# Moving the block loads of chunks 6 and 7 ahead of an output-weight load on the DMA-issuing queue

## The chip, the cores and the metric

The kernel runs on one core of a Trainium2 chip. The core has five engines that run side by side, each through its own list of instructions in order: TensorE (PE; its weight loads appear as PEld), VectorE (DVE), ScalarE (ACT), GpSimd (POOL) and SyncE (SP), which here does nothing but issue DMA transfers. The metric is the device time of one execution in microseconds (us). Less is better.

## What is computed

```python
def _attn_ref(q, k, v):                      # 8 batches, 8 heads, 576 positions, 64 per head
    scores = scale * np.matmul(q, k.transpose(0, 1, 3, 2))
    Dmat = np.where(rel >= 0, gamma[:, None, None] ** rel[None, :, :], 0.0)
    ret = scores * Dmat[None, :, :, :]
    return np.matmul(ret, v).astype(np.float32)

def _moe_ref(x, w1, w2, w3, w_out):          # x: 4608 x 512, w1..w3: 512 x 768, w_out: 768 x 512
    h = np.maximum(np.maximum(x @ w1, x @ w2), x @ w3)
    return (h @ w_out).astype(np.float32)
```

The first part is a retention layer: attention scores without softmax, with a weight that decays with distance by a factor of the head. Its output, with the heads side by side, is the input x of a feed-forward layer that takes the maximum of three products and multiplies it by w_out. The four weights arrive as 64-bit floating-point numbers; the kernel turns them into 32-bit numbers itself.

## The kernel before, in words

**Tiling.** The 4608 rows are cut into 36 chunks of 128 rows, and four chunks make one feed-forward tile of 512 rows, so there are nine tiles. While `ffn(t)` works on the feed-forward tile `t`, the retention steps of the four chunks of tile `t + 1` are woven in. `steps(t + 1)` returns twelve lists of steps, called places here. The loop at the bottom of the kernel runs the steps of one place and then lets `ffn(t)` go on to its next `yield`. There is no automatic scheduling: the order in which these Python functions are called is the order of each engine's instructions.

**The first tile.** Only the first tile, `ffn(0)`, is touched by this change. Its up products run in nine units of two halves each (`up_plain`, PE line 858, four double-pass matmuls of 128x512 a half), and after place n comes unit n. While these run, the weights are converted (`convert`, 12 pairs of pieces: nine pairs of w1 to w3, then three pairs of w_out). A pair needs, in this order, ACT lines 695 and 696, DVE line 703 with ACT lines 702 and 704, then DVE lines 708, 713 and 728. Each raw pair lies in one of four buffers (`bits`); the conversion of a pair ends with the load of further pieces (`load_weights`), which waits for a buffer whose DVE line 713 is done. After the up products come the down products with w_out (`downs_plain`, PE line 845).

**The chunks 4 to 7**, which `steps` calls a, b, c and d, are the ones prepared during `ffn(0)`. What happens to one chunk:

- `load(g, "kv")` issues two DMAs on SP (line 247): `kraw` and `vraw`, 256 KB each.
- `load_blocks(g, 0, 1, 2, 3)` issues sixteen DMAs on SP (line 229): eight 32 KB pieces of `qraw`, then eight of `kxraw`. They write 32x32 blocks in places such that one VectorE transpose of 32x32 blocks turns the chunk. There are two buffers of each, so chunk 7 takes that of chunk 5.
- `transposes(g)` is two DVE instructions (line 216), `kT<-kxraw` and then `qT<-qraw`.
- `decay(g)` multiplies the values by their decay. For chunks 4 and 5 it is one DVE instruction (line 254). For chunks 6 and later it is eight ACT instructions, one a head (line 204, `vraw<-vraw,gk`), put in a list called `scaling` from which `scale(3)` takes three after each half unit.
- `scores(g)` calls `chunk_scores`: for each head, PE line 322 (`sk`, needs `kT` and `qT`) and PE line 325 (`kv`, needs `kraw` and the scaled `vraw` of that head). Before it, whatever is left in `scaling` is issued.
- `values([a, b])` multiplies on (PE lines 439 and 446) and gives the input of the next tile.

**Order around the change.** The second half of unit 8 is followed by `scores(6)`, `scores(7)` and the down products. The sixteen ACT multiplications of chunks 6 and 7 thus go to the ACT queue in groups of 3, 3, 3, 3, 3 and 1, between the conversion's instructions: the third group has the last two of chunk 6 and the first of chunk 7, and the last group has the eighth head of chunk 7 alone.

**SP's queue.** All transfers are issued by SP in order. Each DMA carries one of eight semaphores in turn, so SP does not issue a DMA before the one eight places ahead of it has landed. A DMA that must wait for a buffer holds up all behind it.

## Time and profile before

| what | value |
|---|---|
| median of 3 runs | 740.69 us (738.68 to 741.06) |
| the profiled execution's own time | 739.48 us |
| its span in the profile | 737.8 us |
| PE busy | 731.2 us (99%) |
| DVE busy | 575.3 us (78%) |
| ACT busy | 352.2 us (48%) |
| SP's DMA queue | 58.76 MB, 35.3% of 16 DMA engines |

The span is the time from the first to the last instruction in the profile; 1.7 us of the execution lie around it. Busy times are sums over the whole span, and most of the span is not like the stage that the change touches, which lies between 58 and 96 us. So the stage is read on its own, from the timelines of SP, ACT, DVE and PE. In a timeline a row gives the start in us, the duration, the engine, the line, the operation, what it writes and reads, and how many equal ones stand together ("x8"); "SPq" is SP's issuing. In the chain of work that ended last, a row "DMA kxraw<-in_k_dram" is the time from the issue of that transfer to its landing.

### The profile page before, as it was taken

The page shows a single profiled execution, that of the slowest core. Times are in us where ns is not written, and L with a number is a line of the kernel's source. Part 1 is how long each engine was busy: PE and PEld are TensorE (multiplying, and loading weights), DVE is VectorE, ACT ScalarE, POOL GpSimd, SP SyncE. Part 2 cuts the span into 40 slices and gives each one's busy share as a digit, 9 for nine tenths or more (in the row PEclk, how much of TensorE's full clock was granted, in tenths as well). Part 3 has the DMA queues.
Part 4 walks back from the last instruction along what each step waited for, and adds up shares of the span by engine and source line. Part 5 has one row for each costly group of instructions (what it writes and reads, how often), then busy time and mean ns, then how long its engine had stood idle before and what let it go on. Part 6 is the DMA issues. An engine that isn't in the chain of part 4 may idle for free.

```text
span 737.8 us, 17257 instructions
## 1 busy us (share of the span) xinstructions
PE 731.2 (99%) x6916; PEld 604.5 (82%) x6916; DVE 575.3 (78%) x1050; ACT 352.2 (48%) x734; POOL 37.1 (5%) x43
## 2 busy tenths in 40 slices
PE   9999999999999999999999999999999999999998
PEld 7644546888888888888888888888888888888887
DVE  4899799999886895689658876787768966893676
ACT  4795905554345524544354535543555255424441
POOL 2000010112000100010000000000100010000000
DMA  9878544414251415141424243322514151000001
GB/s 234 270 225 248 113 85 119 83 27 92 70 103 23 95 40 105 36 84 48 102 51 77 47 109 60 65 52 59 114 26 91 44 106 26 1 29 30 1 1 57
DMA packets 234832, 59.90 MB, mean 81 GB/s; under 512 B 220672, under 2 KB 228864, under 8 KB 234752
## 3 DMA queue, kind: packets, MB, share of 16 engines
q1 hardware_dynamic: 233776, 58.76, 35.3%
q8 instruction: 54, 0.88, 0.5%
q14 instruction: 26, 0.21, 0.1%
q10 hardware_dynamic: 976, 0.04, 0.1%
HBM read 49.32 MB, written 9.44 MB: 80 GB/s over the span
## 4 chain that ended last, share of the span: by engine, by line
PE 91%; SPq 5%; DMA 2%; DVE 1%; issue 0%; DVEq 0%
PE a L833 20%; PE b L833 17%; PE c L833 9%; PE di L666 7%; PE d L833 6%; PE e L833 6%; PE dhc L666 5%; PE up L858 3%; PE deg L666 3%; SPq L229 3%; PE sk L322 3%; PE down L845 3%; PE o L439 2%; PE o L446 2%; PE dfd L666 2%; PE dx L573 1%
## 5 line engine op out<-in xcount | busy, mean ns | idle before, releaser
L821 DVE TENSOR_TENSOR part<-part 128x512 f32<-128x512 f32 x168 | 117.8, 701 | 85.9 <-ACT part L818 83.3
L818 ACT COPY part<-b 128x512 f32<-128x512 f32 x120 | 70.3, 586 | 163.2 <-PE b L833 162.7
L821 DVE TENSOR_TENSOR h<-h,part 128x512 f32<-128x512 f32 x120 | 83.2, 694 | 23.8 <-ACT h L818 19.8
L204 ACT ACTIVATE vraw<-vraw,gk 128x64 f32<-128x64 f32 x240 | 77.0, 347 | 11.3 <-DMA vraw<-in_v_dram 11.3
L818 ACT COPY part<-a 128x512 f32<-128x512 f32 x96 | 56.3, 586 | 51.5 <-PE a L833 51.1
L833 PE MATMUL b<-s,n 128*128 128x256 f32 x288 | 73.9, 379 | 0.0
L858 PE MATMUL up<-xT,w 128*128 128x512 f32 (+2 forms) x160 | 62.9, 552 | 0.0
L833 PEld LDWEIGHTS b<-s,n 128*128 128x128 f32 x288 | 54.7, 190 | 7.4
L858 PEld LDWEIGHTS up<-xT,w 128*128 128x128 f32 x160 | 28.8, 190 | 31.5 <-issue 28.6
L339 POOL TENSOR_TENSOR s<-s,gs_of 64x512 f32<-64x512 f32 x24 | 26.4, 1101 | 552.3 <-DVE s L337 512.1
L833 PE MATMUL c<-xT,w 128*128 128x256 f32 x192 | 51.3, 389 | 0.0
L655 ACT COPY k<-di 128x256 f32<-128x256 f32 x49 | 18.3, 373 | 68.5 <-PE di L666 42.1
L833 PE MATMUL d<-s,w 128*128 128x256 f32 x192 | 49.8, 380 | 0.0
L833 PE MATMUL b<-xT,n 128*128 128x256 f32 x192 | 49.3, 379 | 0.0
L833 PE MATMUL a<-xT,w 128*128 128x256 f32 x192 | 49.3, 379 | 0.0
L833 PE MATMUL a<-s,w 128*128 128x256 f32 x192 | 49.3, 379 | 0.0
L833 PE MATMUL a<-xT,n 128*128 128x256 f32 x192 | 45.4, 379 | 0.0
L833 PE MATMUL e<-xT,w 128*128 128x256 f32 x192 | 45.4, 379 | 0.0
L833 PEld LDWEIGHTS e<-xT,w 128*128 128x128 f32 x192 | 36.5, 190 | 5.4 <-issue 0.5
L833 PEld LDWEIGHTS b<-xT,n 128*128 128x128 f32 x192 | 36.5, 190 | 5.0
L833 PEld LDWEIGHTS a<-xT,n 128*128 128x128 f32 x192 | 36.5, 190 | 5.0
L833 PEld LDWEIGHTS a<-xT,w 128*128 128x128 f32 x192 | 36.5, 190 | 5.0
(183 smaller groups left out, 1378.6 us busy)
## 6 DMA issues: line engine op xcount, KB each, us to landing
bits<-in_moe_w_dram SPq DMA_DIRECT2D x9, 1024.0 KB, 7.9
kraw<-in_k_dram SPq DMA_DIRECT2D x32, 256.0 KB, 3.1
vraw<-in_v_dram SPq DMA_DIRECT2D x32, 256.0 KB, 3.9
qraw<-in_q_dram SPq DMA_DIRECT2D x256, 32.0 KB, 2.1
kxraw<-in_k_dram SPq DMA_DIRECT2D x256, 32.0 KB, 2.1
out_dram<-osb SPq DMA_DIRECT2D x56, 128.0 KB, 1.7
bits<-in_moe_w_out_dram SPq DMA_DIRECT2D x6, 512.0 KB, 6.0
out_dram<-osb SPq DMA_DIRECT2D x7, 256.0 KB, 2.0
```

The lines of the kernel that those rows point to most:

```text
L204: scaling.popleft()()
L229: nc.sync.dma_start(t[r:r + 32, :, e, :], src[b, :, pos:pos + 32, 32 * a:32 * a + 32].rearrange("h p i -> p h i"))
L322: nc.tensor.matmul(s[half(c), h, :], lhsT=kT[half(c), h, :], rhs=qT[half(c), h, :], start=True, stop=True)
L339: nc.gpsimd.tensor_tensor(new, new, factor, op=ALU.mult)
L439: nc.tensor.matmul(o[m][half(c), n, u, :], lhsT=vds[g][half(m), h, :], rhs=sts[g][half(m), h, :], start=n == 0 and u == 0, stop=place(g, m ...
L655: nc.scalar.copy(place, a)
L666: nc.tensor.matmul(banks[chain], lhsT=hidden(h, order, b, late_ones)[:, e], rhs=late["V"][v][:, e], start=begins and e == 0, stop=chain no ...
L818: nc.scalar.copy(of[step], ps[step[0]][:])
L821: nc.vector.tensor_tensor(of[dst], a, b, op=op)
L833: nc.tensor.matmul(ps[chain][:, e, :], lhsT=factor(w, 2 * fp + e), rhs=xS[t][x], start=n == 1 and e == 0, stop=ends, skip_group_check=True)
L845: nc.tensor.matmul(b[:], lhsT=h[:, fb, m * P:(m + 1) * P], rhs=w_sb["out", fb], start=fb == blocks[0], stop=fb == blocks[-1])
L858: nc.tensor.matmul(ps[:, a:b], lhsT=w_sb[i, fb][:, dc * P:(dc + 1) * P], rhs=xT[t][:, dc, a:b], start=dc == 0 and a == 0, stop=dc == NDC - ...
```

## The change

The sixteen-DMA block loads of chunks 6 (c) and 7 (d) are moved to the fifth place. Chunk 6's stand at its beginning, ahead of the chunk's own `load`; chunk 7's stand at its end, behind chunk 5's transposes.

```diff
             at(4, (transposes, a))
-            at(5, (load, c, "kv"), (decay, b), (transposes, b))
-            at(6, (load, d, "kv"), (decay, c), (load_blocks, c, 0, 1, 2, 3))
-            at(7, (values, [a, b]), (decay, d), (convert, 2), (load_blocks, d, 0, 1, 2, 3))
+            at(5, (load_blocks, c, 0, 1, 2, 3), (load, c, "kv"), (decay, b), (transposes, b), (load_blocks, d, 0, 1, 2, 3))
+            at(6, (load, d, "kv"), (decay, c))
+            at(7, (values, [a, b]), (decay, d), (convert, 2))
             at(8, (transposes, c))
```

The lists of PE, DVE, ACT and POOL stay the same, instruction for instruction. On SP the order becomes (two DMAs to a pair of w_out or to a `kraw` and `vraw`, sixteen to a set of blocks):

```
before: w_out pair 1 | kv 6 | w_out pair 2 | kv 7 | blocks 6 | w_out pair 3 | blocks 7 | blocks 8 ...
after:  w_out pair 1 | blocks 6 | kv 6 | blocks 7 | w_out pair 2 | kv 7 | w_out pair 3 | blocks 8 ...
```

## The prediction

> **What bounds the kernel now.** I read the page's chain first, then PE's waits over the whole span, then the chain and the timelines between 58 and 96 us.

> ```profile
> ## 4 chain that ended last, share of the span: by engine, by line
> PE 91%; SPq 5%; DMA 2%; DVE 1%; issue 0%; DVEq 0%
> ```

> PE carries the chain; 5% of it is SP's issuing. PE's list of waits says where PE is idle, and from 22 us on it has one entry:

> ```profile
> PE sk L322 <- DVE qT L216: 1.8, 1, 1.8
> ```

> It is the start of `scores(7)`. Everything else PE does behind 22 us stands back to back, so this stage can give back at most 1.8 us, and whatever holds PE here longer is added whole: from 95.42 us the chain is PE alone, matmul behind matmul. The chain (start, duration, what) shows what the 1.8 us come from:

> ```profile
> 81.65 4.72 DMA bits<-in_moe_w_out_dram
> ...
> 90.20 2.31 DMA kxraw<-in_k_dram
> ...
> 92.59 0.71 DVE kT L216
> 93.30 0.60 DVE qT L216
> ```

> The blocks of chunk 7 are issued last of their kind, behind w_out's third pair; the last lands at 92.5, and DVE, idle for 3.1 us before it, transposes. SP's timeline gives the queue:

> ```profile
> 59.15 0.92 SPq L516 DMA_DIRECT2D bits<-in_moe_w_out_dram  x2
> 60.11 0.67 SPq L247 DMA_DIRECT2D kraw<-in_k_dram  x1
> 60.89 1.54 SPq L247 DMA_DIRECT2D vraw<-in_v_dram  x1
> 62.97 4.03 SPq L516 DMA_DIRECT2D bits<-in_moe_w_out_dram  x2
> 67.09 0.38 SPq L247 DMA_DIRECT2D kraw<-in_k_dram  x1
> 67.51 1.47 SPq L247 DMA_DIRECT2D vraw<-in_v_dram  x1
> 69.03 6.65 SPq L229 DMA_DIRECT2D qraw<-in_q_dram  x8
> 75.72 5.39 SPq L229 DMA_DIRECT2D kxraw<-in_k_dram  x8
> 81.21 0.87 SPq L516 DMA_DIRECT2D bits<-in_moe_w_out_dram  x2
> 82.13 4.58 SPq L229 DMA_DIRECT2D qraw<-in_q_dram  x8
> 86.75 3.90 SPq L229 DMA_DIRECT2D kxraw<-in_k_dram  x8
> ```

> SP issues without a pause here, so what is moved forward pushes back what it passes. The change moves 32 issues past two w_out pieces and the `kraw` and `vraw` of chunk 7 (and sixteen of them past those of chunk 6). So the question is who uses these four, and when. `vraw` of chunk 7 lands 6.5 us after its issue at 67.51 (the answer on that one issue), at 74.1. Its first user is on ACT:

> ```profile
> 80.91 0.81 ACT L204 ACTIVATE vraw<-vraw,gk 128x64 f32<-128x64 f32 x3
> 81.63 1.13 ACT L695 ACTIVATE expo<-bits 128x1024 f32<-128x1024 bf16 x1
> 82.67 1.25 ACT L696 ACTIVATE mant<-bits,one 128x1024 f32<-128x1024 uint32 x1
> ...
> 89.65 0.35 ACT L204 ACTIVATE vraw<-vraw,gk 128x64 f32<-128x64 f32 x1
> ```

> The third multiplication of the first row, near 81.4, is chunk 7's first head; the last row, done at 90.0, is its eighth. Between them ACT is never idle: 8.6 us of work in a fixed order, conversion and multiplications alternating. PE's last `kv` matmuls of `scores(7)` need the eighth. The cover of `vraw` 7 is thus 81.4 - 74.1 = 7.3 us on ACT's side.

> **The change, part by part.** Nothing is computed that was not before, and only SP's order differs. I follow SP's clock.

> *Blocks 6 forward.* They come right behind w_out's first pair (59.15, 59.65). There is no wait for their buffer: chunk 4's transposes end at 53.9 (53.20 + 0.67, DVE). The situation is that of 81.21 in the queue above: seven issues go out, the eighth waits for the second w_out piece to land (eight semaphores), and the `kxraw` take 3.9. That piece lands 7.1 us after 59.65, at 66.7 as before. So the `kxraw` go from 67.1 to 71.0.

> *`kraw` and `vraw` 6 back,* from 60.11 and 60.89 to 71.1 and 71.6. Where they follow blocks elsewhere (99.59 and 100.09) they take 0.40 and 0.53 and land 3.0 and 3.4 us later: `vraw` 6 lands at 75.0. ACT wants it at 72.33, so ACT is 2.6 us late. Cover: the conversion of the last up pair, which has its weights ready at 78.1 (DVE line 728, 76.83 + 1.23) for a unit that PE starts at 84.1 (91.1 less 7.0); 2.4 us late it is still 3.6 us early. Cost on PE: nothing.

> *Blocks 7 forward.* They wait for chunk 5's transposes, which end at 61.8; SP gets there at 72.2, so the wait costs nothing, and what is queued behind it (w_out's second pair, `kraw` and `vraw` 7) is held by the sixteen issues, not by DVE. Sixteen issues behind a `kraw` and `vraw` take 7.8 us at the pace of 0.49 (3.89 + 3.90 at 119.52) to 9.7 (5.73 + 3.90 and the gap, at 128.57). In the trace of before one issue at 76.72 takes 1.92 instead of 0.45, beside the 112 small matmuls of `values` (PE, 75.17 to 77.19); those stay where they are, within this set. I take 9.4: the set ends at 81.6. All of it lands by 83.7, 8.8 us earlier than before.

> *w_out's second pair and `kraw`, `vraw` 7 back.* The pair is issued at 81.65 and 82.1, `kraw` at 82.55, `vraw` at 83.0 (67.51 before). A pair at 81.21 landed 3.8 and 4.7 us after its issues; so the second piece is there at 86.8. `kraw` and `vraw` 7 landed 0.9 and 1.8 us behind that piece when they followed it directly (73.2 and 74.1 against 72.3). So `vraw` 7 lands at 88.6, 14.5 us later than before, and its cover of 7.3 is gone.

> [...]

> *What this does to ACT, DVE and PE.* ACT reaches chunk 7's first head at 83.7 (81.1 + 2.6) and stands until 88.6. The eighth head is done 8.6 us later, at 97.2; with the last `kv` matmuls behind it the down products start at 97.6 instead of 95.42: **2.2 us later**.
> The transposes that the change sets free from their blocks do not come earlier either: DVE's line 708 stands ahead of them, and it needs ACT line 696, which ends 2.5 us behind the first head, at 91.2. With 1.2 for line 708, 0.6 for a maximum and 1.3 for the transposes that makes 94.3, against 93.9 before. So PE stands for about 2 us ahead of `scores(7)`, runs seven heads, and stands again for the eighth.

> *w_out's third pair* goes from 81.21 to 83.5 and lands near 91.2 (two pieces of about 1.3 us each behind `vraw` 7); ACT wants it at 88.6 + 6.1 = 94.7. Covered. The w_out products on DVE end at 96.9 and 106.6 in the profile for down matmuls that begin at 104.5 and near 111.5; both move by no more than 2 us, as PE does. *Blocks 8* move from 90.75 to about 89, and cost nothing.

> Sum: -1.8 (old wait) and +4.0 (new ones) is +2.2 us on the profiled execution, 739.48 to 741.7. That execution lies 1.2 us under the median of the runs, so on the median 740.69 + 2.2 = 742.9. Bounds: with the quick pace `vraw` 7 lands at 87.0 (+0.6); with 9.7 and another long issue of 1.5 it is issued at 84.75 and, at the 6.5 us of the row at 67.51, lands at 91.3 (+4.8).

> **Rivals.** Differences up to 0.3% (2.2 us) are about what a measurement of this kernel can tell from no change; the forecast stands on that line.

> *The wait just goes* (faster). If `vraw` 7 is in place by 84.6, ACT is at most 3.2 us late, the eighth head is done at 93.2, chunk 7's transposes at 90.3, and `scores(7)` follows `scores(6)` without a gap: -1.8 us at the best, 738.9. It decides at a landing of 86.4: in the trace the eighth head's `kv` matmuls run near 95.2, and less 8.6 and 0.2 for the hand-over that is where ACT must begin; below, a gain. For it: the blocks' wait is real and is cured. Against it: between 66.7 and `vraw` 7's issue lie 25 block issues at 0.49, two pieces of w_out and three of `kraw` and `vraw`; even the bound of 87.0 misses it.

> *A draw.* `vraw` 7 lands between 86 and 87: the new wait takes the old one's place exactly, 740.7 within 0.6 us.

> *PE's rate falls behind the gaps* (slower still). At the start of the kernel PE is slow: four transposes (`kt`, line 286) give way to the next after 0.92 us at 4.02 and after 0.50 at 8.44, so from its first matmul at 1.12 to the 5.85 at which the slow rows end, 4.7 us, it runs at about half its rate. Should two gaps of 2 us with 1 us of small matmuls between them bring that back for as long, the down matmuls behind lose half of 4.7, 2.4 us: +4.6, 745.3. Against it: behind the present gap of 1.8 us sixteen down records take 7.06 and the next 32 take 13.93, the same rate, and the granted clock of the windows is 1.00.
> [...]

> **How the numbers follow.** The new wait on `vraw` 7 (+0.6 to +4.8): 0.68. Rate loss: 0.12. Draw: 0.11. Wait gone: 0.09. The likeliest gives 742.9, its own range is 741.3 to 745.5. For 8 in 10 I reach down into the draw and most of the gain, 739.8, and up to 745.6. Slower by over 0.3%: 0.39 from the upper part of the forecast and 0.12 from the rate loss, 0.51. Faster by over 0.3%: the gain's best is 0.24%, so only its luckier part, 0.05. The rest, 0.44, lies within.

> **What would show it.** In the profile after: SP issues w_out's second pair near 81.6 and `vraw` 7 near 83; ACT has a wait at line 204 on `vraw<-in_v_dram` of about 5 us that ends near 88.6, and a smaller one near 75; PE's waits name ACT `vraw` L204 at `kv` L325; the down products start near 97.6; nothing waits for `kxraw`. I am wrong if ACT shows no wait there or one that ends before 86.4, if the down products start before 95.4, or if the difference arises behind 96 us, where I expect a plain shift.

## The result, and the profile after

The changed kernel takes 746.15 us (median of 7 runs, 743.07 to 746.57); the kernel before, run beside it, 740.69 (median of 7, 737.94 to 741.51). The ratio is 1.0076, with a 95% interval of 1.0058 to 1.0095: **slower by 5.5 us**, where 2.2 were forecast, and 0.55 us above the upper end of the range. The profiled execution of the changed kernel took 746.22 us, so it stands for the median; its span is 744.5 us and its mean granted clock 0.995, against 1.00 in the profile of before. (The granted clock is the share of its full speed at which TensorE ran.)

The chain of the page hardly differs. ACT has taken 1% of it:

```profile
## 4 chain that ended last, share of the span: by engine, by line
PE 91%; SPq 4%; DMA 3%; ACT 1%; issue 1%; DVE 0%
```

PE's waits over the whole span have two entries in the stage where there was one of 1.8:

```profile
PE sk L322 <- DVE qT L216: 2.5, 1, 2.5
PE kv L325 <- ACT vraw L204: 1.6, 1, 1.6
PE kt L286 <- DMA kraw<-in_k_dram: 1.5, 1, 1.5
```

The first is the start of `scores(7)`, the second its eighth head. The third lies near 18 us, ahead of everything that the change touches; it was 0.38 us in the profile of before (its timeline at 17.15), and so this execution reaches its first up product (PE line 858) at 22.9 instead of 21.9 us. That 1.0 us is not the change's and is taken off below.

SP's timeline, in the new order:

```profile
60.76 0.92 SPq L516 DMA_DIRECT2D bits<-in_moe_w_out_dram  x2
61.73 7.36 SPq L229 DMA_DIRECT2D qraw<-in_q_dram  x8
69.13 3.91 SPq L229 DMA_DIRECT2D kxraw<-in_k_dram  x8
...
73.64 0.53 SPq L247 DMA_DIRECT2D vraw<-in_v_dram  x1
74.26 4.12 SPq L229 DMA_DIRECT2D qraw<-in_q_dram  x8
78.43 4.65 SPq L229 DMA_DIRECT2D kxraw<-in_k_dram  x8
83.17 0.87 SPq L516 DMA_DIRECT2D bits<-in_moe_w_out_dram  x2
...
84.56 0.58 SPq L247 DMA_DIRECT2D vraw<-in_v_dram  x1
```

`vraw` of chunk 7 is issued at 84.56 instead of 67.51, behind both sets of blocks and w_out's second pair. ACT's timeline shows what that does:

```profile
85.91 0.57 ACT L204 ACTIVATE vraw<-vraw,gk 128x64 f32<-128x64 f32 x2
90.02 0.35 ACT L204 ACTIVATE vraw<-vraw,gk 128x64 f32<-128x64 f32 x1 [3.53 <-DMA vraw<-in_v_dram]
90.27 1.15 ACT L695 ACTIVATE expo<-bits 128x1024 f32<-128x1024 bf16 x1
...
98.30 0.33 ACT L204 ACTIVATE vraw<-vraw,gk 128x64 f32<-128x64 f32 x1
```

The third group of multiplications is split. Its two for chunk 6 run at 85.91, the one for chunk 7's first head stands 3.53 us until `vraw` lands, and the eighth head follows 8.6 us later. In DVE's timeline the transposes of chunk 7 are later than before although their blocks are there, because line 708 stands ahead of them and waits for ACT:

```profile
92.59 1.23 DVE L708 SCALAR_TENSOR_TENSOR mant<-frac,mant 128x1024 f32<-128x1024 int32 x1 [0.97 <-ACT mant L696]
93.73 0.68 DVE L863 TENSOR_TENSOR h<-h,up 128x512 f32<-128x512 f32 x1
94.33 0.70 DVE L216 STREAM_TRANSPOSE kT<-kxraw 128x512 f32<-128x512 f32 x1
94.95 0.67 DVE L216 STREAM_TRANSPOSE qT<-qraw 128x512 f32<-128x512 f32 x1
```

The chain that leads into the down products, and goes on behind them, first in the profile of before, then in this one:

```profile
95.42 7.06 PE down L845 x16
...
104.51 13.93 PE down L845 x32
```

```profile
84.56 5.43 DMA vraw<-in_v_dram
...
98.39 0.25 ACT vraw L204
98.68 0.48 PE kv L325 x4
99.16 9.82 PE down L845 x16
...
111.02 13.93 PE down L845 x32
```

Two things are to be seen here. The down products start at 99.16 instead of 95.42, 3.74 later. And the first sixteen, the same instructions as before, take 9.82 us instead of 7.06; the next 32 take 13.93 as they did. A table by stretches (stretch, its length, busy time of PE, PEld, DVE, ACT and POOL with the number of instructions, the granted clock, then the DMA share and GB/s) shows where the 2.76 us come from:

```profile
91.04:94.45 3.41, 2.26 (x67) 1.21 (x65) 2.44 (x5) 3.38 (x7) 0.00 (x0) 1.00 0.58 156
94.45:97.86 3.41, 1.28 (x60) 1.16 (x60) 3.38 (x5) 3.41 (x6) 0.00 (x0) 1.00 0.30 45
97.86:104.69 6.83, 6.01 (x11) 2.79 (x12) 6.07 (x9) 3.59 (x7) 2.30 (x2) 0.50 0.67 128
104.69:111.00 6.31, 6.31 (x139) 3.56 (x138) 4.30 (x5) 0.43 (x2) 0.19 (x1) 1.00 0.43 70
```

From 97.86 to 104.69 the granted clock is 0.50. The sum: 3.74 later, less the 1.0 of the late start, is 2.7 from the two waits; 2.76 from the halved clock; together 5.5, as the difference of the medians. That the two agree to a tenth is luck: these two executions differ by 6.7 us (746.22 less 739.48), and how much of it belongs to the start can be set at 1.0 or, by SP's list, at 1.6 (see below).

### The profile page after: what moved, and what is told of

It reads as the page before. It is cut to its first block, busy times and chain, and to the rows that moved or that the text cites. A ratio compares the mean times of both kernels' runs of the same rounds, so it can differ in the third digit from the quotient of the medians.

```text
span 744.5 us, 17259 instructions
## 1 busy us (share of the span) xinstructions
PE 734.1 (99%) x6916; PEld 605.5 (81%) x6916; DVE 576.0 (77%) x1050; ACT 352.3 (47%) x734; POOL 37.2 (5%) x43
## 4 chain that ended last, share of the span: by engine, by line
PE 91%; SPq 4%; DMA 3%; ACT 1%; issue 1%; DVE 0%
PE a L833 19%; PE b L833 17%; PE c L833 9%; PE di L666 6%; PE d L833 6%; PE e L833 6%; PE dhc L666 5%; PE up L858 3%; PE deg L666 3%; PE down L845 3%; PE sk L322 3%; SPq L229 3%; PE o L439 2%; PE o L446 2%; PE dfd L666 2%; PE dx L573 1%
## 5 line engine op out<-in xcount | busy, mean ns | idle before, releaser
L204 ACT ACTIVATE vraw<-vraw,gk 128x64 f32<-128x64 f32 x240 | 77.0, 347 | 10.7 <-DMA vraw<-in_v_dram 6.7
L833 PEld LDWEIGHTS a<-s,w 128*128 128x128 f32 x192 | 36.5, 190 | 5.0
```

What stands on the lines that cost most here:

```text
L204: scaling.popleft()()
L833: nc.tensor.matmul(ps[chain][:, e, :], lhsT=factor(w, 2 * fp + e), rhs=xS[t][x], start=n == 1 and e == 0, stop=ends, skip_group_check=True)
```

## The experiments

Each kernel ran 6 to 12 times beside the kernel before; ratios are to that. Its medians in the four groups of runs were 740.51 (with both gaps filled, with the decay on GpSimd, with blocks 6 alone, and with blocks 7 behind `vraw`), 739.68 (one gap filled, and the two with chunk 6's `load` ahead of its blocks), 740.50 (the four with chunk 3's `kraw` earlier) and 740.51 (the three with the start filled).

### Are there two costs? Unread matmuls in both gaps

Nine matmuls whose result nobody reads ahead of `scores(7)` and six ahead of its eighth head; otherwise the changed kernel. They keep PE busy while it would wait.

```diff
+    def fill_pe(n):
+        ps = ps_y.tile([P, P], FP32, tag="y", name="fill_ps")
+        for _ in range(n):
+            nc.tensor.matmul(ps[:], lhsT=ident[:], rhs=ident[:], start=True, stop=True)
...
         for h in range(H):
+            fillers.pop(g)() if h == H - 1 and g in fillers else None
...
-                        scores(d)
+                        fill_pe(9), fillers.update({d: partial(fill_pe, 6)}), scores(d)
```

> The change as it is, with matmuls of the identity that nobody reads put into PE's two gaps: nine ahead of chunk 7's scores and six ahead of its eighth head (about 0.23 us each, so about 2.1 and 1.4 us). SP, ACT and DVE stay as in the change. Theory: the waits remain (down products start 2.5 to 3 us later than before) but PE keeps its rate: 16 down records take 7.1 us again, granted clock 1.00, time 743.2 to 743.8, about 2.8 us under the change. Rival two (the rate falls for another reason than idle PE): 746, 9.8 us for the 16 records.

Measured: 743.14 us, ratio 1.0033 [1.0015, 1.0051]; the granted clock was 1.00 or 0.999 in all 12 runs. Its chain (start, duration, what):

```profile
99.30 7.06 PE down L845 x16
```

The down products start as late as in the changed kernel (99.30 against 99.16; first up product at 23.1 and 22.9), yet run at full rate. So 3.0 us (746.15 less 743.14) come from PE standing idle, not from the time at which it goes on, and SP's transfers, whose order is the same in both, are not the reason for the lost rate. The 2.6 us that are left above the median of the kernel before are the waits. They are 3.3 us if the kernel before is counted by its 20 runs of this group with a clock of 0.999 or more (median 739.89), since its other 15 lost rate too.

### Is it ACT's queue? Chunk 7's decay on GpSimd

The changed kernel, with the eight ACT multiplications of chunk 7 made one GpSimd instruction, so that nothing on ACT needs `vraw` 7.

```diff
-        if CPT <= g < CPT + 2:
+        if CPT <= g < CPT + 2 or g == 2 * CPT - 1:
             vds[g] = t
-            nc.vector.tensor_tensor(t[:], t[:], factor, op=ALU.mult)
+            (nc.gpsimd if g == 2 * CPT - 1 else nc.vector).tensor_tensor(t[:], t[:], factor, op=ALU.mult)
```

> The change, with chunk 7's values multiplied by their decay on GpSimd in one instruction (three of that kind took 1.04 us each in the kernel before) instead of eight on ACT between the conversion's. vraw 7 still lands near 88.5 to 90. Theory: ACT no longer waits for it; it waits for w_out pair 2 only (landing 87 to 88), so chunk 7's transposes run near 92.5 and its scores near 93.5 to 94.5; one gap of 1.5 us, no rate loss, down products start within 1 us of the kernel before: 739.7 to 740.9. Rival one (kv 6 moved back): that wait stays, 743 or more. Rival two: 742 to 743, with the slow 16 records.

Measured: 740.43 us, ratio 0.9986 [0.9966, 1.0006]. GpSimd's timeline, then PE's waits of the stage, of this kernel:

```profile
89.72 1.08 POOL L254 TENSOR_TENSOR vraw<-vraw,gk 128x512 f32<-128x512 f32 x1 [19.59 <-DMA vraw<-in_v_dram]
```

```profile
PE sk L322 <- DVE qT L216: 1.1, 1, 1.1
```

`vraw` lands nearly as late as in the changed kernel (89.6 against 90.0), and the whole loss is gone. The late landing costs only through the fixed order of ACT's list, where 8.6 us of work, most of it conversion, stand between the first head and the eighth. That ACT has eight instructions less to run is not the reason: on the kernel before with blocks 6 alone moved, the same edit brought nothing (741.12 against 740.81 us, both with chunk 3's `kraw` earlier, further down). That this kernel beats the one before can't be said: its interval holds 1.

### Which of the two gaps? One filled at a time

The same matmuls as above, in one place only: the nine ahead of `scores(7)`, or the six ahead of its eighth head.

```diff
-                        scores(d)
+                        fill_pe(9), scores(d)
```

> The change with only PE's first gap filled (nine unread matmuls of the identity ahead of chunk 7's scores); the second gap of about 1.6 us, ahead of the eighth head, stays. If the rate drops because two gaps and the thin matmuls between them fall into one short stretch, one gap of 1.6 us, like the 1.8 us of the kernel before, leaves the rate alone: clock 1.00 in nearly all runs, 743.1 as with both filled. If each gap above some 1.5 us already brings the drop, 745 to 746.

Measured: 742.93 us, ratio 1.0034 [1.0020, 1.0048]. PE's one wait left in the stage is 1.4 us at `kv` L325; 2 of 12 runs had a clock of 0.997 to 0.998, the others 0.999 or 1.00. Its profile starts early (first up product 21.7) and its down products at 97.1.

```diff
-                        scores(d)
+                        fillers.update({d: partial(fill_pe, 6)}), scores(d)
```

> The change with only PE's second gap filled (six unread matmuls ahead of the eighth head); the first gap of about 2.5 us ahead of chunk 7's scores stays. If it takes both gaps: clock 1.00, 743.1. If the longer gap alone is enough: clock 0.995 to 0.998 and 744.5 to 746.

Measured: 743.88 us, ratio 1.0049 [1.0031, 1.0068]. The wait left is 1.9 us at `sk` L322. Of 11 runs six had a clock of 0.997 or 0.998 (median 744.8), the other five 0.999 or more (742.3). None of these 23 runs was at 0.995, as five of the changed kernel's seven were (the other two at 0.998): neither gap alone brings the whole drop. Whether one alone brings a smaller one is not shown. No run of low clock was profiled here, the kernel before itself was at 0.998 in 8 of its 27 runs of this group (a 28th, of 1968.9 us, is left out), and one profile further down (blocks 7 behind chunk 7's `vraw`) has a drop of 3.41 us at the start of the kernel, from 18.38 to 21.79.

### One set of blocks at a time

Blocks 6 alone moved to the fifth place; blocks 7 stay at the seventh.

```diff
-            at(5, (load, c, "kv"), (decay, b), (transposes, b))
-            at(6, (load, d, "kv"), (decay, c), (load_blocks, c, 0, 1, 2, 3))
+            at(5, (load_blocks, c, 0, 1, 2, 3), (load, c, "kv"), (decay, b), (transposes, b))
+            at(6, (load, d, "kv"), (decay, c))
```

> One half of the change alone: chunk 6's blocks at the fifth place, chunk 7's stay at the seventh, behind w_out pair 3 (order: w_out pair 1, blocks 6, kv 6, w_out pair 2, kv 7, w_out pair 3, blocks 7). Theory: vraw 7 lands near 80 and costs nothing, the blocks of chunk 7 land near 87 instead of 92.5, so the old wait of 1.8 us is mostly gone: 739.0 to 739.8. Rival one (moving kv 6 back costs): 743. Rival two (the rate falls without gaps): 742.

Measured: 740.05 us, ratio 0.9993 [0.9975, 1.0010]. PE's wait at `scores(7)` is 0.7 instead of 1.8, so blocks 6 do no harm and 1.1 us of the old wait go, but no gain can be measured. In its profile the first up product comes at 22.9, 1.0 later than in the profile of before, and the down products at 95.4, as then: the shorter wait was taken up by a later start. 739.0 to 739.8 was expected, and that gain did not come.

The changed kernel with blocks 7 behind chunk 7's `kraw` and `vraw`, which keep their place near 76:

```diff
-            at(5, (load_blocks, c, 0, 1, 2, 3), (load, c, "kv"), (decay, b), (transposes, b), (load_blocks, d, 0, 1, 2, 3))
-            at(6, (load, d, "kv"), (decay, c))
+            at(5, (load_blocks, c, 0, 1, 2, 3), (load, c, "kv"), (decay, b), (transposes, b))
+            at(6, (load, d, "kv"), (decay, c), (load_blocks, d, 0, 1, 2, 3))
```

> The change with one thing undone: chunk 7's blocks stand behind its kraw and vraw (order: w_out pair 1, blocks 6, kv 6, w_out pair 2, kv 7, blocks 7, w_out pair 3). Theory (the lateness of vraw 7, through ACT's queue, opens two gaps on PE, and PE's rate halves behind them): vraw 7 lands near 80, before ACT reaches its first head at about 84, so no wait on it; chunk 7's transposes are no longer late by their blocks; the down products start 1.3 to 1.8 us earlier than in the kernel before and at the full rate: 738.9 to 739.4. Rival one (the loss comes from moving kraw and vraw 6 back, which holds ACT for 4 us at 73): that wait stays here, so 743 or more. Rival two (the rate drop has nothing to do with the gaps and comes with the denser DMA traffic): 16 down records still take about 9.8 us, 742.

Measured: 742.50 us, ratio 1.0025 [1.0006, 1.0043]. The expectation was missed. ACT's timeline of this kernel shows a wait that it had left out:

```profile
91.81 0.81 ACT L204 ACTIVATE vraw<-vraw,gk 128x64 f32<-128x64 f32 x3
94.90 1.18 ACT L695 ACTIVATE expo<-bits 128x1024 f32<-128x1024 bf16 x1 [2.28 <-DVE qT L216]
95.98 1.21 ACT L696 ACTIVATE mant<-bits,one 128x1024 f32<-128x1024 uint32 x1
97.10 0.33 ACT L204 ACTIVATE vraw<-vraw,gk 128x64 f32<-128x64 f32 x1
```

Chunk 7's `vraw` is there in time and no row of ACT waits for it. But now w_out's third pair stands behind blocks 7; it is issued at 88.66 and lands at 94.80, and its conversion (L695 at 94.90) stands ahead of the eighth head. (The row names DVE; the landing of the pair is the later event, 0.1 us ahead of the start.) PE waits 1.2 us for that head, and the down products start at 97.8. Moving one set past a w_out pair makes the same kind of wait as moving it past `vraw`, from another transfer. How much of the 2.0 us it costs is not shown: in this execution PE is late from the start (first up product at 24.8), which hides a part of the wait, and its only drop of the clock ahead of the kernel's end lies there, from 18.38 to 21.79.

### Rivals for the cause that fell

**ACT's first wait.** In the changed kernel ACT also stands 3.92 us, until 77.36, for chunk 6's values. With chunk 6's `load` ahead of its blocks:

```diff
-            at(5, (load_blocks, c, 0, 1, 2, 3), (load, c, "kv"), (decay, b), ...
+            at(5, (load, c, "kv"), (load_blocks, c, 0, 1, 2, 3), (decay, b), ...
```

> The change with kraw and vraw of chunk 6 put back ahead of chunk 6's blocks (order: w_out pair 1, kv 6, blocks 6, blocks 7, w_out pair 2, kv 7, w_out pair 3). ACT's first wait, near 73, goes; chunk 7's vraw still lands at 88 to 90. Theory (vraw 7 sets it): as the change, 745 to 746.5, with ACT's wait on vraw 7 longer by what the first one was shorter. Rival (the first wait costs a good part): 743.5 or less.

Measured: 746.24 us, ratio 1.0077 [1.0052, 1.0103], as the change itself. ACT now only stands longer for chunk 7's first head, 8.11 us until 90.42, and its eighth is as late as in the changed kernel (98.67 against 98.30). The first wait is not the cause.

The same swap without blocks 7's move (the kernel before, with blocks 6 right behind chunk 6's `load`):

> The kernel before with one move: chunk 6's blocks directly behind its kraw and vraw, everything else in its old order (w_out pair 1, kv 6, blocks 6, w_out pair 2, kv 7, w_out pair 3, blocks 7). Theory: neither vraw 6 (landing near 70) nor vraw 7 (near 81) holds ACT, w_out pair 3 lands near 86 to 88, chunk 7's blocks land 3 to 5 us earlier than in the kernel before, so its old wait of 1.8 us shrinks to 0.5 or less and PE keeps its rate: 738.8 to 739.6, below both. Rival (SP is so full that chunk 7's blocks land no earlier): 740.5.

Measured: 739.78 us, ratio 1.0004 [0.9985, 1.0023]: nothing gained or lost, where a gain to 738.8 to 739.6 was expected.

**The start of the kernel.** Both costs could have come from a late start near 18 us, which differs from run to run. First the wait there was attacked by issuing chunk 3's `kraw` ahead of the first weights, in four kernels: before, after, before with blocks 6 alone, and the last with chunk 7's decay on GpSimd too.

```diff
-    load(2, "kq")
+    load(2, "kq"), load(CPT - 1, "k")
...
-    load(CPT - 1, "kqv")
+    load(CPT - 1, "qv")
```

> The kernel before with one move at its very start: chunk 3's kraw is issued ahead of the first 1 MB of w1. PE's wait for it near 17 us (0.4 to 2.5 us in the nine profiles so far, different from run to run) should go. If that wait is what makes some runs of the kernel before slow (at 2.0 and 2.5 us the clock record shows 3.4 us at half rate right behind it), the time is 738.7 to 739.3 with clock 1.00 in nearly all runs and a narrower spread. If the spread has another source: 739.5 to 740.5 and clocks down to 0.995 as before.

> The change with the same move at the start, so that the start's share of the spread is out of the comparison. Theory (two gaps at chunk 7's scores of about 4 us together, 2.2 to 2.7 us more than before, and 1.7 to 2.8 us of half rate behind them): 743.5 to 744.7, that is 4.5 to 5.5 us above the kernel before with this move, clock 0.995 to 0.998. If part of the change's loss came from the start: 742.5 or less.

> Chunk 6's blocks alone at the fifth place, with the move at the start. The wait at chunk 7's scores was 0.7 us in that order's profile against 1.8 in the kernel before: 1 us below the kernel before with the same move, 737.7 to 738.3, and 2 us below the kernel before as it was. If the orders of the blocks make no difference once the start is settled: the same as it, 738.7 to 739.3.

> As the former, and chunk 7's values multiplied on GpSimd in one instruction. ACT then has eight instructions less ahead of chunk 7's transposes, but DVE's conversion stands ahead of those too: 0 to 0.7 us less than the former, 737.3 to 738.3. If ACT is no longer what the transposes wait for: no difference.

Measured, in this order: 741.05 us (1.0003 [0.9986, 1.0020]), 745.99 (1.0072 [1.0051, 1.0093]), 740.81 (0.9999 [0.9985, 1.0012]), 741.12 (1.0004 [0.9986, 1.0021]). The edit missed its aim; PE's wait at the start only moved to another row, as the waits of the first of the four show:

```profile
PE kv L368 <- POOL vd L262: 3.0, 1, 3.0
```

What stands is that the change costs as much as ever on this other start, and that blocks 6 alone, or with the decay moved, gain nothing measurable. One of the six runs of the changed kernel with this start kept a clock of 1.00, and it took 743.04 us, as with both gaps filled; the other five, at 0.993 to 0.995, took 745.57 to 747.86.

Then the start was filled instead, with six unread matmuls ahead of chunk 3's transposes on PE, in three kernels: before, after, and before with blocks 6 alone.

```diff
-    transposes(CPT - 1, "k")
+    fill_pe(6), transposes(CPT - 1, "k")
```

> The kernel before with six unread matmuls of the identity (about 1.35 us) ahead of chunk 3's key transposes, where PE waits 0.4 to 2.5 us for data. If half rate behind that start wait is what parts the slow from the quick runs of the kernel before (739.5 at clock 1.00, 741 to 742 at 0.998), clocks are 1.00 in nearly all runs and the median is 739.0 to 739.8; where the wait is shorter than the filling, the later wait of 1.8 us at chunk 7's scores takes up the difference. If the spread comes from elsewhere, clocks of 0.998 stay in a third of the runs and the median is 740.5 to 741.

> The change with the same six matmuls at the start. If the change's low clock comes from its gaps near 93 to 99 us alone, it stays at 0.995 to 0.998 and the time at 745 to 746.5. If the start had a part in it: 743.5 to 744.5, clock 0.998 to 1.00.

> Chunk 6's blocks alone at the fifth place, with the same six matmuls at the start. Its own wait at chunk 7's scores was 0.7 us, so it is up to 1 us quicker than the kernel before with the filled start where the start is early, and equal where it is late: 738.2 to 739.5.

Measured: 740.69 us (1.0005 [0.9977, 1.0032]), 746.14 (1.0061 [1.0036, 1.0086]), 740.27 (0.9985 [0.9959, 1.0011]). With the start filled, the changed kernel still has a clock of 0.995 in 11 of 12 runs, and in its profile the stretch of half clock begins at 98.35, behind its own two gaps (PE's waits there: 4.4 and 1.2), and of the down records from 101.0 on the slowest takes 1.22 us, against a median of 0.59. So its low clock is not the start's. On the kernel before the filling changed nothing: 4 of 12 runs still had a clock of 0.998 or less, against 12 of 29 without it. So these runs give no sign that its lost rate comes from that wait. The gain expected for blocks 6 (738.2 to 739.5) did not come.

No kernel here beat the kernel before by more than its interval.

## Why the prediction was too low

**SP's queue: right.** Every stage of the list was 1.6 us later than computed, beginning with w_out's first pair (60.76 against 59.15), and the paces were those of the rows: `vraw` 7 was issued at 84.56 (83.0 + 1.6 = 84.6) and landed at 90.0 (88.6 + 1.6 = 90.2). The shift arises ahead of all that the change touches: SP issues the same weight piece at 28.56 instead of 26.82, behind longer issues from 10.93 on (one `qraw` takes 5.22 us instead of 3.39).

**The landing.** From the first piece of the pair (83.17) to `vraw` 7 it took 6.8 us, against 6.95 in the sum from the rows.

**ACT, DVE and PE: right.** ACT's wait ends at 90.02, the eighth head is done 8.6 us later at 98.63, DVE's line 708 holds the transposes back (they end at 95.62; 94.3 was computed, 95.9 with the shift of 1.6), PE's list names ACT `vraw` L204 at `kv` L325, and nothing waits for `kxraw`. Two sizes were off, both without effect on the end: ACT's earlier wait ended at 77.36 instead of near 75, and since ACT therefore came to chunk 7's first head at 86.5 instead of 83.7 (84.0 by the 81.4 of its own row), it stood 3.5 us there instead of 5. The step "2.2 us later" is 3.74 in the profile, 2.7 less PE's late start, and 2.1 less the 1.6 by which SP's list was late; in the runs with both gaps filled it is 2.6 (743.14 less 740.51). The two profiles with one gap filled, which start early (first up product at 21.7 and 22.1), have their down products at 97.2 and 97.7; 97.6 was forecast.

**The step that failed** is the one on PE's rate. The prediction had the mechanism and nearly its price (2.4 against 2.76 us), but set it beside the forecast as a rival with a chance of 0.12, when the forecast itself made the two gaps from which it follows. Had it been a term of the sum, the sum would have been 4.6, and with both terms as measured 4.9 to 5.5. Its argument was drawn from a place that couldn't carry it: the trace of before, in which a single gap of 1.8 us leaves the clock at 1.00. One execution with one gap shows no rule for two, and here a wait of 2.5 us, small matmuls and the start of one of 1.6 came ahead of the drop. The row of 94.45 to 97.86 has PE busy for 1.28 of 3.41 us: the last 1.3 us of the first gap, the small matmuls of seven heads, and the second gap up to there add up.

**"A plain shift behind 96 us"** was named as what would make the prediction wrong if it failed, and it is what failed: of the 6.5 us by which the next 32 down products are later than before (111.02 against 104.51), 2.76 arise behind 97.86.

**The old wait's 1.8 us** were counted as a gain in every branch. In the runs that shorten it alone (0.7 instead of 1.8 with blocks 6 moved) nothing could be measured. The wait is as long as PE is early: in the profile of the kernel before with the start filled, the first up product comes at 23.15 instead of 21.90, PE does not wait at `scores(7)` at all, and the down products start at 95.07 instead of 95.42. So the 1.8 us belong to the one early execution that was profiled; how long the wait is in the median run was not settled.

## What to carry to other kernels

Before a transfer is moved forward in a single queue, look up the first user of each transfer that it passes, and what else stands behind that user in its engine's order: here a 256 KB load with 7.3 us of cover held up a list in which 8.6 us of unrelated work lay between its first and its last use. Two short waits on TensorE close together are not to be priced one by one: here waits of 2.5 and 1.6 us left PE busy for only 1.28 of 3.41 us, 6.83 us at a clock of 0.50 followed, and they cost 2.76 us beside the waits. Where idle time comes as close together, put such a loss into the sum. A few unread matmuls in such gaps tell how much of a loss is waiting (here 2.6 us) and how much is the clock (3.0). And a wait behind which PE only catches up with a transfer is no gain in store: look whether it is still there in an execution that comes to it later.

## What the runs showed of the hardware

```profile
14.96:18.38 3.42, 1.64 (x26) 1.27 (x22) 1.73 (x5) 1.74 (x3) 0.78 (x1) 1.00 0.79 182
18.38:21.79 3.41, 3.23 (x34) 2.93 (x36) 2.67 (x4) 2.73 (x5) 0.83 (x2) 0.50 0.93 275
```

```profile
92.93:96.34 3.41, 1.96 (x62) 1.91 (x63) 3.38 (x6) 3.38 (x6) 0.00 (x0) 1.00 0.45 71
```

```profile
16.27:19.68 3.41, 1.79 (x36) 1.46 (x34) 3.28 (x7) 3.25 (x6) 1.62 (x2) 1.00 0.82 184
```

Busy shares of 0.38 (1.28 of 3.41) and 0.48 (1.64 of 3.42) were followed by half clock, 0.57 and 0.52 were not. In the changed kernel 0.56 (1.92 of 3.42, from 15.94), 0.66 (2.26 of 3.41, from 91.04) and, at its end, 0.49 (1.67 of 3.41, from 739.57) were not either: the stretches right behind them have 1.00. So the border in these rows is near a half, 0.48 on one side of it, 0.49 and 0.52 on the other; they are too few to set it closer. Whether a given gap crosses it would then hang on how it falls on the grid; that is the author's inference, and fits the kernel with the change and chunk 3's `kraw` earlier, in which the same program kept a clock of 1.00 in one run and had 0.993 to 0.995 in five. That it is the busy share, and not some other count of PE's work, was read from these traces and not tested by itself. The kernel before loses some clock too: pooled over all groups, 48 of its 120 runs had a clock of 0.998 or less, with the median time 2 us higher at 0.998 and 5 us at 0.995. None of those was profiled, so where they lose it stays open. The old gap may be one place: in the profile of before, PE is busy for only 1.65 of the 3.41 us from 92.00 to 95.41, a share of 0.48, should the grid fall there.
